# Loading the last pair's two wide tiles of x beside the next layer's first passes

## The chip, the cores and the metric

The kernel runs on one core of a Trainium2 chip. The metric is the device time of one execution in microseconds (us), lower is better. The engines have their own instruction queues and run them in order: TensorE (PE, matrix products into PSUM banks), VectorE (DVE), ScalarE (ACT), GpSimd (POOL, here mostly an issuer of DMAs) and SyncE (SP, an issuer of DMAs only).

## The reference

Two layers of a Fourier mixing and two of a gated feed-forward, in turn, on x of 2048 rows by 512 columns in float32:

```python
def mix(x):    # x: [S=2048, D=512]
    a = x @ dft_hid_re.T;  b = x @ dft_hid_im.T
    return dft_seq_re @ a - dft_seq_im @ b
def geglu(x):  # w_gate, w_up: [512, 1792], w_down: [1792, 512]
    return (gelu(x @ w_gate) * (x @ w_up)) @ w_down
for layer in range(4):
    n = (x - mean(x)) / sqrt(var(x) + 1e-5)      # per row
    x = x + (mix(n) if layer % 2 == 0 else geglu(n))
```

## The kernel before

**Products.** Each float32 operand is split into two halves, `hi` and `lo`: ACT copies `hi` (line 170), DVE subtracts to get `lo` (line 172). One product is then three matmuls of 128x128 by 128x512, `hi*hi`, `hi*lo` and `lo*hi` (lines 227, 228, 229). Large products are done by a seven-product scheme (names such as S1 to S4, T1 to T4, A11, A22, P1 to P7), so DVE also forms many sums and differences (lines 203, 207, 210, and 198 and 196 for negated splits).

**Stages.** A mixing layer takes the 2048 rows of the sequence transform in four blocks of 512 rows (`NB` is 4). For each block the stages A11, A12, S2 and S4 multiply the transform's tiles by the normalized rows; `s2` and `s4` run the last two. In the second mixing (layer 2) blocks are paired, (0, 1) and (2, 3), and the hidden transform is done once for a pair, as products P1 to P7 (`pair_product`). P1, P2, P4 and P7 run between the stages of the pair's blocks. The other three, P6, P5 and P3, four steps each, are the twelve entries of `PAIR_REST`. For the first pair they run beside stage S2 of block 2 (`s2` calls `pair_rest` at every second of its steps). For the last pair they are put on the list `spare`, and layer 3 takes them off one by one between its own first gate and up products (`up` calls `beside_mix` six times for each index n, so the twelve run beside the first two indices).

**The wide tiles.** The result of a pair product comes out transposed. DVE turns it back (`turned_into`, lines 865 and 210) and adds it to x, which lies in SBUF in a matching layout: one tile of 128x2048, 1 MB, for each block of a pair. The tile of the pair's first block is called `xwide` and that of the second `wide`. `pair_wide_load` fills one from DRAM with four DMAs of 256 KB on SP's queue (line 977), and `pair_out` writes it back with four on POOL's (line 980). Each name has one buffer. `xwide` is free long before the last pair. `wide` is also used for the normalized rows that the next layer turns: it is written by DVE (line 782), stored to a DRAM tile `t` by POOL (line 785), and `t` is fetched back in another layout by 16 small POOL DMAs for each half of the rows (line 796).

**What sets the order.** The code is written in the order of the work, and a scheduler places the instructions on each engine's queue with the help of its own timing model. All weights and transform tiles run through one stream (`items`, `load_next`, `take`): SP loads a tile into one of 98 slots `s` as soon as the slot's earlier tile has been read (line 350, or 1345 for prepared pieces of the gate and up weights, `wb`). A load on SP's queue that waits for its slot holds all loads behind it. Loads named `ws` are tiles of the sequence transform, `wq` pieces of the hidden transform for the pair products, `wb` and `wc` pieces of the feed-forward weights.

**The table that is changed.** `WIDE_AT = 14, 5` holds the step of `s2` and the step of `s4` of the last block at which `xwide` and `wide` are loaded. The other pair loads its two tiles in `pair_groups`, which the change leaves alone.

Of the kernel before, what the change touches and what calls it, by code (L numbers as in the profile page):

```python
# [20 lines left out]
NB = S // TB  # L21
# [5 lines left out]
MORE = 8  # L27
RAW = 4
FETCHING = 2
WIDE_AT = 14, 5  # L30
IN_ORDER = (3, 0),
HELD = {0: (1, 2, 3), 2: ()}
WARM = 12
# [33 lines left out]
def fnet_geglu(ctx: ExitStack, tc: tile.TileContext, x_in, ws, wh, wgu, wdn, wdc, whc, out):  # L67
# [53 lines left out]
    class Slots:  # L121
# [20 lines left out]
        def lend(self, tile, name):  # L142

            self.lent.add(name)
            self.free += [(tile[:, i * 512:(i + 1) * 512], name) for i in range(NT)]
# [17 lines left out]
    def behind(engine):  # L163
        return tc.issue_after(bank_read[engine].ins) if in_order[0] and engine in bank_read else ExitStack()
# [36 lines left out]
    def minus(out, a, b):  # L201
        with behind("DVE"):
            nc.vector.tensor_tensor(out, a, b, op=ALU.subtract)  # L203
# [652 lines left out]
    def moved(wide, outside, run):  # L856
        view = outside.rearrange("(j t) (p e) -> p t j e", t=32, e=P)
        for p in range(NT):
            v = wide[p * 32:(p + 1) * 32]
            run(v.rearrange("t (j e) -> t j e", e=P), view[p])  # L860
# [15 lines left out]
    def mix(layer):  # L876
# [58 lines left out]
        paired = {b for p in PAIRED.get(layer, ()) for b in p}  # L935
        by_pair = {b: p for p in PAIRED.get(layer, ()) for b in p}
        xu, xv, pair_banks, kept_p, pair_wide, late_v, sums_due, pair_now = {}, {}, {}, {}, {}, {}, [], [()]

        def arrived(b, m, c):
            if b not in paired:  # L940
                return
            t = cs.pop((m, c))
            if b == by_pair[b][0]:
                assert c not in (xv if m else xu)
                (xv if m else xu)[c] = t
                cs["P2" if m else "P1", c] = t
                return
            if m:
                cs["P4", c] = late_v[c] = t
            else:  # L950
                v = cs["P7", c] = sb.get(lasting=True)
                minus(v, xu[c], t)
                cs["u", c] = t
            if ("u", c) in cs and c in late_v:
                v = cs["P5", c] = cs.pop(("u", c))
                minus(v, v, late_v[c])
                read_once(c, late_v.pop(c))
                sums_due.append(c)

        def pair_sums():  # L960
            c = sums_due.pop(0)
            u, v = xu.pop(c), xv.pop(c)
            minus(u, cs["P5", c], u)
            with behind("DVE"):
                nc.vector.scalar_tensor_tensor(v, v, -1.0, u, op0=ALU.mult, op1=ALU.subtract)
            cs["P6", c], cs["P3", c] = u, v

        def pair_wide_load(b, n):
            pool = tpool if n else upool
            if b >= NB - 2:  # L970
                order = tc.issue_after(stream["last"].ins)
            else:
                order = ExitStack()
            assert not sb.out("z" if n else "x")
            pair_wide[n] = pool.tile([P, NT * D], F32, name="wide" if n else "xwide")
            with order:
                moved(pair_wide[n], xs[layer, b], lambda v, rows: nc.sync.dma_start(v, rows))
# [7 lines left out]
        def pair_product(name, k):  # L985
            bank = "P6" if name in ("P5", "P3") else name
            if bank not in pair_banks:
                pair_banks[bank] = [ps8.get() for _ in range(2)]
            ps = pair_banks[bank]
            (hi, lo), w = take()  # L990
            for c in range(2):
                cut = slice(c * P, (c + 1) * P)
                mm3(ps[c], (w[:, half[0]][:, cut], w[:, half[1]][:, cut]), (hi, lo), FIRST.get(name) == k, LAST[name] == k)
            sb.put(hi, lo, w)
            if LAST[name] == k:
                pair_ended(name, ps)
# [24 lines left out]
        def first_sum(c):  # L1021
            t, other = kept_p["P1"][c], kept_p["P2"][c]
            plus(t, t, other)
            turned_into(pair_wide[0], c, t)
            sb.put(t, other)

        def pair_rest(i):
            if sums_due:
                pair_sums()
            if i in FIRST_SUMS:  # L1030
                first_sum(FIRST_SUMS.index(i))
            pair_product(*PAIR_REST[i])
# [108 lines left out]
        def s2(b):  # L1141
            last = b == NB - 1
            if b == 0:
                lend("z")
                lend("x")
            cs.update(cs_next)
            cs_next.clear()
            for c in range(2):
                arrived(b, 0, c)
            chain = chain_banks.pop(b)  # L1150
            if b not in paired:
                x_banks(layer, b)
            one, three = [ps8.get() for _ in range(2)], [ps8.get() for _ in range(2)]
            sides[b] = one, three
            if last:
                late = later.pop("norms late", [])
                queue.extend(late + [None] * (FETCH_AT - len(late) if paired else 14) + [run for fetch in later.pop("fetches") for run in (None, fetch)])
            for j, (i, k) in enumerate(skewed(3)):
                if rest_beside(layer, b) and j % BESIDE == 0:
                    pair_rest(j // BESIDE)  # L1160
                    if j == len(skewed(3)) // 2:
                        stream["more"] = FURTHER
                if last and paired and j == WIDE_AT[0]:
                    pair_wide_load(NB - 2, 0)
                if i == 0:
                    six(chain, "T2", k, False, k == NK - 1)
                elif i == 1:
                    six(one, "T1", k, k == 0, k == NK - 1, "T12" if last else None)
                else:
                    six(three, "T3", k, k == 0, k == NK - 1)  # L1170
                if i == 0 and k == SEED_AT and b not in paired:
                    hid_banks[b] = x_seeded(b, range(2))
                if k < NK - 1:
                    continue
                if i == 0:
                    down_pieces(b, 1)
                    us[b] = [copied(p, b in paired) for p in chain]
                    ps8.put(*chain)
                    if b not in paired:
                        hid_banks[b] += x_seeded(b, range(2, NT))  # L1180
                for c in range(2):
                    if i == 1:
                        v = cs[1, 2 + c] = sb.get(lasting=b in paired)
                        plus(v, us[b][c], one[c])
                    elif i == 2:
                        plus(cs[1, 2 + c], cs[1, 2 + c], three[c])
                if i == 2:
                    for c in range(2):
                        arrived(b, 1, 2 + c)

        def s4(b):
            last = b == NB - 1
            if b == (1 if paired else NB - 4):
                sb.reclaim("z")
                if paired:
                    sb.reclaim("x")
            stream["more"] = 0
            one, three = sides.pop(b)
            u = us.pop(b)
            for j, (i, k) in enumerate(skewed(2)):  # L1200
                if last and paired and j == WIDE_AT[1]:
                    pair_wide_load(NB - 1, 1)
                if i == 0:
                    six(one, "B22", k, False, k == NK - 1, "22" if last else None)
                else:
                    six(three, "T4", k, False, k == NK - 1, "T34" if last else None)
                    if paired and b >= NB - 2:
                        for _ in range(-(-len(chores) // hid_left[0]) if chores else 0):
                            chores.pop(0)()
                        hid_left[0] -= 1  # L1210
                if k < NK - 1:
                    continue
                if i == 0:
                    down_pieces(b, 2)
                for c in range(2):
                    if i == 0:
                        v = cs[0, 2 + c] = sb.get(lasting=b in paired)
                        plus(v, u[c], one[c])
                    else:
                        plus(u[c], u[c], three[c])  # L1220
                        cs[1, c] = u[c]
                for c in range(2):
                    arrived(b, i, c if i else 2 + c)
            ps8.put(*one, *three)
# [653 lines left out]
```

## Time and profile before

| what | value |
|---|---|
| median of 3 runs | 1612.08 us (1611.62, 1612.08, 1616.12) |
| the profiled execution, own time | 1612.12 us |
| its span, first to last instruction | 1610.3 us |
| mean granted TensorE clock | 0.994 |
| PE busy | 1592.9 us, 99% of the span |
| DVE, ACT, POOL busy | 1189.7, 880.8, 315.6 us |
| DMA | 432.80 MB, mean 269 GB/s |
| the last pair's loads of x issued | `xwide` from 1112.8 us, `wide` from 1147.1 us |

The span is cut short by 1.8 us against the execution's own time, and that time equals the median within 0.1 us. A busy PE is not a PE at its peak: matmul records overlap, so stretches are compared below by how many matmuls were issued in them. Times in the profile are counted from the first instruction. "SPq" is SP issuing DMAs; a row's duration there is the time it spent issuing, not the time of the transfer.

### The profile page before, as it was taken

To read this page: it belongs to the slowest core of one execution; us is meant where nothing else is said; L and a number is where in the kernel's file an instruction comes from. 1 tells how busy PE (TensorE), PEld (TensorE's weight loads), DVE (VectorE), ACT (ScalarE), POOL (GpSimd) and SP (SyncE) were. 2 spreads that over 40 slices of the span, in tenths; PEclk is the share of its full clock that TensorE was granted. 3 is DMA by queue.
4 is the path that set the end of the run, shared out by engine and by line. 5 is a ranking of instruction groups with operands and counts; after the bars stand their busy time and mean duration, and the time that the engine had idled before them with its cause. 6 is when DMAs were issued, how large, how long until landed. Compare 5 with 4: busy or idle time off the path is not lost. (4 is left out here: it accounts for less than half of the span.)

```text
span 1610.3 us, 22765 instructions
## 1 busy us (share of the span) xinstructions
PE 1592.9 (99%) x6960; PEld 1311.8 (81%) x6960; DVE 1189.7 (74%) x2082; ACT 880.8 (55%) x1687; POOL 315.6 (20%) x533
## 2 busy tenths in 40 slices
PE   9999999999999999999999999999989999999999
PEld 7888888888888888888888888887768888888887
DVE  7997888878699784675878875998875556843574
ACT  8955565654767644656567543534542565433460
POOL 4122332341456102330040000022301000000000
PEclk9999999999999999999999999999889999999999
DMA  9888999976998899997786758789868958895445
GB/s 358 293 329 314 332 318 345 334 260 199 343 322 318 267 333 314 326 353 225 273 303 199 262 166 206 240 279 271 236 231 285 280 171 252 302 293 188 131 144 157
DMA packets 245019, 432.80 MB, mean 269 GB/s; under 512 B 29024, under 2 KB 72288, under 8 KB 243872
## 3 DMA queue, kind: packets, MB, share of 16 engines
q1 hardware_dynamic: 212208, 328.82, 63.6%
q0 software_dynamic: 30000, 100.43, 17.4%
q10 hardware_dynamic: 2688, 2.10, 0.5%
q8 instruction: 55, 0.90, 0.2%
q14 instruction: 68, 0.56, 0.1%
HBM read 333.97 MB, written 97.26 MB: 268 GB/s over the span
## 5 line engine op out<-in xcount | busy, mean ns | idle before, releaser
L228 PE MATMUL p<-s,s 128*128 128x512 f32 x2304 | 897.2, 390 | 0.6 <-DVE s L172 0.5
L229 PE MATMUL p<-s,s 128*128 128x512 f32 x2304 | 891.5, 390 | 3.5 <-DMA s<-wb 3.5
L227 PE MATMUL p<-s,s 128*128 128x512 f32 x2304 | 852.5, 391 | 8.3 <-ACT s L170 3.7
L170 ACT ACTIVATE s<-s 128x512 fp32r<-128x512 f32 (+1 forms) x852 | 480.4, 608 | 305.7 <-DVE s L203 69.7
L172 DVE TENSOR_TENSOR s<-s,s 128x512 fp32r<-128x512 f32 (+1 forms) x852 | 537.6, 663 | 119.5 <-ACT s L170 101.5
L227 PEld LDWEIGHTS p<-s,s 128*128 128x128 f32 x2304 | 434.2, 189 | 100.7 <-ACT s L170 4.7
L229 PEld LDWEIGHTS p<-s,s 128*128 128x128 f32 x2304 | 434.4, 189 | 94.1 <-DMA s<-wb 3.9
L228 PEld LDWEIGHTS p<-s,s 128*128 128x128 f32 x2304 | 434.1, 188 | 92.8 <-DVE s L172 2.2
L207 DVE TENSOR_TENSOR s<-s,p 128x512 f32<-128x512 f32 x211 | 142.3, 682 | 163.7 <-PE p L229 133.5
L203 DVE TENSOR_TENSOR s<-s,s 128x512 f32<-128x512 f32 (+1 forms) x399 | 234.6, 609 | 5.8 <-DMA s<-ws 3.2
L214 ACT ACTIVATE s<-p 128x512 f32<-128x512 f32 x234 | 135.6, 592 | 112.9 <-PE p L229 110.8
L1355 ACT ACTIVATE s<-s 128x512 f32<-128x512 f32 x84 | 52.8, 628 | 46.3 <-DVE s L207 45.9
L336 POOL DMA_DIRECT2D wb<-s x84 | 46.1, 550 | 86.2 <-ACT s L170 68.4
L1355 ACT ACTIVATE s<-p 128x512 f32<-128x512 f32 x28 | 16.7, 596 | 83.1 <-PE p L229 81.5
L689 ACT ACTIVATE s<-s,shift,rstd 128x512 f32<-128x512 f32 x61 | 48.8, 810 | 18.3 <-DVE shift L656 10.4
L1371 DVE TENSOR_TENSOR s<-s,p 128x512 f32<-128x512 f32 x56 | 38.3, 683 | 24.8 <-PE p L229 24.8
L980 POOL DMA_DIRECT2D x<-wide x8 | 5.2, 658 | 231.1 <-DVE wide L210 231.1
L221 ACT ACTIVATE p<-p 128x512 f32<-128x512 f32 x56 | 32.6, 584 | 31.6 <-PE p L229 31.4
L170 ACT ACTIVATE s<-xwide 128x512 fp32r<-128x512 f32 (+1 forms) x56 | 34.3, 618 | 27.9 <-DVE xwide L207 10.4
L210 DVE TENSOR_TENSOR s<-s,s 128x512 f32<-128x512 f32 (+1 forms) x61 | 36.4, 603 | 17.1 <-DMA s<-ws 12.4
L172 DVE TENSOR_TENSOR s<-xwide,s 128x512 fp32r<-128x512 f32 (+1 forms) x56 | 37.4, 676 | 15.3 <-ACT s L170 15.1
L666 POOL TENSOR_SCALAR rstd<-rstd 128x1 f32<-128x1 f32 x32 | 19.8, 619 | 108.1 <-ACT s L665 98.8
(96 smaller groups left out, 675.1 us busy)
## 6 DMA issues: line engine op xcount, KB each, us to landing
s<-ws SPq DMA_DIRECT2D x368, 256.0 KB, 5.0
s<-wb SPq DMA_DIRECT2D x294, 256.0 KB, 5.0
s<-wc SPq DMA_DIRECT2D x182, 256.0 KB, 4.4
wb<-s POOLq DMA_DIRECT2D x98, 256.0 KB, 4.6
s<-wq SPq DMA_DIRECT2D x56, 256.0 KB, 4.5
s<-x SPq DMA_DIRECT2D x52, 256.0 KB, 5.4
s<-wh SPq DMA_DIRECT2D x52, 256.0 KB, 5.6
wc<-s POOLq DMA_DIRECT2D x49, 256.0 KB, 5.4
```

The lines of the kernel that those rows point to most:

```text
L170: newest["ACT"] = nc.scalar.activation(hi, src, AF.Copy)
L172: newest["DVE"] = nc.vector.tensor_tensor(lo, src, f32(hi), op=ALU.subtract)
L203: nc.vector.tensor_tensor(out, a, b, op=ALU.subtract)
L207: bank_read["DVE"] = nc.vector.tensor_tensor(out, a, b, op=ALU.add)
L214: bank_read["ACT"] = nc.scalar.activation(v, src, AF.Copy)
L227: nc.tensor.matmul(ps, ah, bh, start=start, stop=False, skip_group_check=True)
L228: nc.tensor.matmul(ps, ah, bl, start=False, stop=False, skip_group_check=True)
L229: newest["PE"] = nc.tensor.matmul(ps, al, bh, start=False, stop=stop, skip_group_check=True)
L336: nc.gpsimd.dma_start(a, f32(t))
L689: nc.scalar.activation(z, x, AF.Identity, bias=shift, scale=rstd)
L1355: nc.scalar.activation(t, g, AF.Gelu_apprx_tanh)
L1371: nc.vector.tensor_tensor(t, t, v, op=ALU.mult)
```

## The change

The two loads leave `s2` and `s4` of the last block. `pair_rest` issues them instead, for the last pair alone: `WIDE_AT = 0, 2` now holds entries of `PAIR_REST`. At entry 0 the tile `wide` is loaded, at entry 2 the tile `xwide`. `wide` is first used when P6 ends (entry 3), `xwide` at entry 9.

```diff
-WIDE_AT = 14, 5
+WIDE_AT = 0, 2
...
         def pair_rest(i):
             if sums_due:
                 pair_sums()
+            if pair_now[0][1] == NB - 1 and i in WIDE_AT:
+                which = 1 - WIDE_AT.index(i)
+                pair_wide_load(pair_now[0][which], which)
             if i in FIRST_SUMS:
...
-                if last and paired and j == WIDE_AT[0]:
-                    pair_wide_load(NB - 2, 0)
...
-                if last and paired and j == WIDE_AT[1]:
-                    pair_wide_load(NB - 1, 1)
```

The number of instructions of each kind is the same before and after. In the rows below a name such as `s69_12677` is slot 69 and a running number, which differs between the two programs; `x2_2` and `x2_3` are the rows of x of the last pair's blocks in DRAM.

SP's queue in stage S2 of the last block, before:

```order
L350 DMA s94_12650<-wq0_181 128x512
L977 DMA xwide_12672<-x2_2_94 32x16x128 x4
L350 DMA s69_12677<-wq1_182 128x512
L350 DMA s86_12576<-ws 128x512
L350 DMA s18_12689<-ws3_0_3_176 128x512
```

and now:

```order
L350 DMA s94_12650<-wq0_181 128x512
L350 DMA s69_12672<-wq1_182 128x512
L350 DMA s18_12684<-ws3_0_3_176 128x512
L350 DMA s86_12576<-ws 128x512
L350 DMA s44_12819<-ws 128x512
```

The four loads of `xwide` no longer stand ahead of the transform tile in slot 86.

SP's queue in stage S4 of the last block, before:

```order
L350 DMA s76_12894<-ws 128x512
L977 DMA wide_12946<-x2_3_95 32x16x128
L350 DMA s34_12919<-ws 128x512
L977 DMA wide_12946<-x2_3_95 32x16x128 x3
L350 DMA s62_12966<-wq3_184 128x512
L350 DMA s83_12978<-wq2_183 128x512
```

and now:

```order
L350 DMA s76_12889<-ws 128x512
L350 DMA s34_12914<-ws 128x512
L350 DMA s62_12956<-wq3_184 128x512
L350 DMA s83_12968<-wq2_183 128x512
L350 DMA s66_12988<-wq3_184 128x512
```

The four loads of `wide` are gone from between the transform's last tiles and the weights of the pair products.

SP's queue where layer 3's weights are loaded, before:

```order
L1345 DMA s23_13111<-wb0_185 128x512
L350 DMA s2_13140<-wq0_181 128x512
L1345 DMA s96_13132<-wb1_186 128x512
L350 DMA s56_13146<-wq1_182 128x512
L350 DMA s27_13164<-wq2_183 128x512
L350 DMA s58_13182<-wq3_184 128x512
L350 DMA s85_13273<-wq0_181 128x512
L350 DMA s36_13296<-wc0_122 128x512
```

and now (one line less in the file from here on, so that line 1345 reads 1344):

```order
L1344 DMA s23_13101<-wb0_185 128x512
L1344 DMA s86_13123<-wb1_186 128x512
L350 DMA s2_13130<-wq0_181 128x512
L350 DMA s27_13154<-wq2_183 128x512
L350 DMA s56_13136<-wq1_182 128x512
L1344 DMA s96_13122<-wb1_186 128x512
L350 DMA s58_13172<-wq3_184 128x512
L977 DMA wide_13263<-x2_3_95 32x16x128 x4
L350 DMA s85_13268<-wq0_181 128x512
L350 DMA s36_13291<-wc0_122 128x512
```

The loads of `wide` now stand behind six other loads that follow the piece of `wb0` in slot 23, which layer 3's first product reads. The four of `xwide` follow eight loads later, behind the next `wq` pieces. The scheduler also moved some neighbours by a few places on PE, DVE and ACT between about 1117 and 1250 us; the largest such move on SP is a piece of `wb0` in slot 5, which now stands ahead of six loads that it stood behind.

## The prediction

> **What bounds the kernel now.** I read the page first, then PE's waits, then PE stretch by stretch, then the queues around each loss.
>
> ```profile
> span 1610.3 us, 22765 instructions
> ...
> PE 1592.9 (99%) x6960; PEld 1311.8 (81%) x6960; DVE 1189.7 (74%) x2082; ACT 880.8 (55%) x1687; POOL 315.6 (20%) x533
> ...
> PEclk9999999999999999999999999999889999999999
> ```
>
> PE is busy all along, so time can only be won where PE waits or its clock falls. The clock falls in two of the 40 slices, numbers 29 and 30 (1127 to 1208 us). PE's waits from 960 to 1300 us (total, times, longest):
>
> ```profile
> PE p L227 <- ACT s L170: 3.7, 2, 3.3
> PE p L229 <- DMA s<-wb: 3.5, 1, 3.5
> PE p L227 <- ACT s L214: 2.3, 1, 2.3
> PE p L227 <- DMA s<-wb: 1.6, 1, 1.6
> PE p L228 <- DVE s L172: 0.5, 1, 0.5
> ```
>
> These 11.6 us lie in three places, which I call A, B and C. The windows give PE's busy time with its matmul count, DVE's, the clock and the DMA share:
>
> ```profile
> 1124.24:1137.55 13.31, 9.50 (x23) 6.28 (x22) 9.50 (x21) 6.31 (x10) 7.34 (x12) 0.62 0.66 192
> 1137.55:1170.44 32.89, 32.89 (x147) 27.22 (x145) 31.05 (x52) 18.19 (x34) 9.30 (x17) 1.00 1.00 272
> 1170.44:1182.24 11.80, 6.67 (x19) 4.70 (x18) 10.28 (x18) 3.29 (x6) 0.00 (x0) 0.71 0.87 315
> 1191.78:1198.88 7.10, 4.84 (x15) 3.49 (x13) 5.90 (x10) 4.34 (x9) 0.00 (x0) 0.76 0.28 80
> ```
>
> A count includes one or two matmuls that straddle the edges. The undisturbed second window gives 32.89 / 145 = 0.227 us for a matmul. A holds 21 matmul starts, worth 4.76 us, so 8.55 of its 13.31 are lost; B holds 18 (4.08), so 7.72 are lost; C holds 13 (2.95), so 4.15 are lost. Together that is 20.4 us, more than the waits, because a slow clock follows them:
>
> ```profile
> 1124.01 0.61 PE L227 MATMUL p<-s,s 128*128 128x512 f32 x2
> 1127.88 1.22 PE L227 MATMUL p<-s,s 128*128 128x512 f32 x2 [3.25 <-ACT s L170]
> ...
> 1130.16 0.63 PE L228 MATMUL p<-s,s 128*128 128x512 f32 x1
> ...
> 1132.58 0.80 PE L228 MATMUL p<-s,s 128*128 128x512 f32 x1 [0.52 <-DVE s L172]
> ...
> 1172.47 0.47 PE L227 MATMUL p<-s,s 128*128 128x512 f32 x1 [1.65 <-DMA s<-wb]
> ```
>
> A record lasts 0.63 in the slow stretch behind A's wait, and 0.47 right behind the wait of 1.65, where the clock has not fallen yet.
>
> **The change, part by part.** SP issued the moved loads here:
>
> ```profile
> 1112.79 2.02 SPq L977 DMA_DIRECT2D xwide<-x  x4
> ...
> 1115.53 25.96 SPq L350 DMA_DIRECT2D s<-ws  x14
> ...
> 1148.03 1.49 SPq L977 DMA_DIRECT2D wide<-x  x3
> 1149.62 4.78 SPq L350 DMA_DIRECT2D s<-wq  x5
> ...
> 1160.88 3.27 SPq L1345 DMA_DIRECT2D s<-wb  x4
> ...
> 1166.99 5.06 SPq L1345 DMA_DIRECT2D s<-wb  x8
> ```
>
> The chain that ended last runs, in this part, through four transfers (start, duration):
>
> ```profile
> 1115.53 10.24 DMA s<-ws
> ...
> 1149.23 8.88 DMA s<-t
> ...
> 1158.40 6.38 DMA s<-t
> ...
> 1171.73 5.35 DMA s<-wb
> ```
>
> *A: xwide leaves S2.* The `ws` tile issued at 1115.53, right behind `xwide`, lands at 1125.77. DVE waits for it:
>
> ```profile
> 1120.59 0.14 DVE L651 TENSOR_SCALAR rstd<-mv 128x1 f32<-128x1 f32 x1
> 1125.86 0.69 DVE L210 TENSOR_TENSOR s<-s,s 128x512 f32<-128x512 f32 x1 [5.13 <-DMA s<-ws]
> ```
>
> The splits behind that sum are what PE waits for. The landings of `xwide` and of `wide` from their issues (shortest, median, longest):
>
> ```profile
> DMA to landing us min/median/max: 4.1/5.6/6.9
> ...
> DMA to landing us min/median/max: 4.7/6.9/11.8
> ```
>
> The first piece of `xwide` lands at 1112.8 + 4.1 = 1116.9, the last at 1114.3 + 6.9 = 1121.2: 1.45 us a piece, 5.8 for four. Without them the `ws` tile lands at about 1120.0; DVE is free for it at 1120.7. DVE's 5.13 goes, and with it PE's 3.25 and the slow stretch. What stays: the split that ended the 0.52 wait comes at 1132.5 - 5.1 = 1127.4, while PE, running on from 1124.24, is there 9 matmuls later, at 1126.3. So 1.1 of the 8.55 stays: A gives 7.4. Bounds: 0, if the small fetches of `t` hold the `ws` tile up as much, and 8.55. I take 7.4, since 5.8 is read from the pieces themselves.
>
> *B: wide leaves S4.* SP's queue was held by it:
>
> ```profile
> SPq L1345 <- DMA wide<-x: 4.0, 1, 4.0
> ```
>
> The last piece was issued at 1149.0 and landed 11.8 later, at 1160.8, just when SP issued the next `wb`. So the rush of `wb` loads from 1160.88 to 1172 starts late, and the one from which the chain goes over to PE lands at 1171.73 + 5.35 = 1177.08. That landing gains on three accounts. DVE and with it the slots, the stores and the fetches of `t` come 5.1 earlier, from A. The transfers lose 1 MB, at least 5.8 us by the price above (by the spread of the landings, 1151.8 to 1160.8 for the last three, up to 12). And four loads fewer stand ahead of it. Together 10.9 at least: it lands at 1166.2 or earlier. PE wants it at 1170.9 now, two matmuls behind the third window's start, and at 1163.5 with A's 7.4 gone. So 0 to 2.7 of B's 7.72 stay; I take 0.5, near the low end, because the price of 5.8 is the lower of the two: B gives 7.2. PE is then 14.6 early.
>
> *C follows.* PE waits for a copy that stands on ACT behind eight splits:
>
> ```profile
> 1179.23 0.58 ACT L221 ACTIVATE p<-p 128x512 f32<-128x512 f32 x1 [7.24 <-PE p L229]
> ...
> 1189.61 4.27 ACT L170 ACTIVATE s<-s 128x512 fp32r<-128x512 f32 x8
> ```
>
> They pile up because ACT sat for 7.24 us behind a copy that waited for PE in B. With B gone the pile goes, but DVE feeds the last of these splits, and DVE is the next bound. The feeding instruction, and DVE's waits just ahead of it:
>
> ```profile
> 1180.38 0.69 DVE L172 TENSOR_TENSOR s<-s,s 128x512 fp32r<-128x512 f32 x1 [0.99 <-ACT s L170]
> 1181.60 0.69 DVE L172 TENSOR_TENSOR s<-s,s 128x512 fp32r<-128x512 f32 x1 [0.53 <-ACT s L170]
> ...
> 1186.17 0.69 DVE L172 TENSOR_TENSOR s<-s,s 128x512 fp32r<-128x512 f32 x1 [1.47 <-ACT s L170]
> 1186.78 0.69 DVE L965 SCALAR_TENSOR_TENSOR s<-s,s 128x512 f32<-128x512 f32 x1
> ```
>
> It can come earlier by 5.13, these 3.0, and the 1.84 that DVE idles in the second window: 10.0, so it ends at 1177.5, and a split of 0.6 and the copy of 0.6 at 1178.7. PE, 14.6 early, wants the copy at 1192.0 - 14.6 = 1177.4, one matmul behind the fourth window's start. A wait of 1.3 stays; behind the 1.65 the clock had not fallen yet, so I charge no slow stretch. C gives 4.15 - 1.3 = 2.8 (bounds 0 and 4.15).
>
> *The new place.* Eight DMAs and some 4 us of issuing (2.02 for `xwide`, as much for `wide`) now stand on SP among loads for later products:
>
> ```profile
> 1188.00:1200.00 12.00, 9.74 (x36) 7.55 (x35) 10.60 (x19) 8.32 (x17) 0.00 (x0) 0.86 0.50 150
> 1209.16 1.25 DVE L210 TENSOR_TENSOR wide<-wide,s 128x512 f32<-128x512 f32 x2
> ```
>
> The DMA engines are half idle there, and the first sum into `wide` comes at 1209.16, near 1193 when PE and DVE run 16 early. `wide` is issued behind the `wb` rush, which ended at 1172 and ends near 1162 now (10.9 earlier); allowing a few more us for the `wq` loads between, and the longest landing, 11.8, it is there by about 1177. The cover is some 16 us. Cost 0; bounds 0 and 7.7, another B. On POOL nothing is moved past. I set 1.0 aside for waits as small as the 0.5 in the list.
>
> Sum: 7.4 + 7.2 + 2.8 - 1.0 = 16.4. Against the profiled execution's own 1612.1 (0.0 from the median), that is **1596 us**.
>
> [...]
>
> **The rivals.** *The chain holds B (1607 us).* PE gains A, arrives early and waits for `wb` all the more, since everything that the landing hangs on moves only with DVE: gain 5.1, 1607.0. For it: DVE is busy 31.05 of 32.89 in the second window and PE's operands come through it. Against it: SP's 4.0 wait on `wide`, which is no DVE time. Between this and the forecast lies a partial gain, 1600 to 1607.
>
> *The loads were not the cause (1612 us).* If the fetches of `t` and the other loads fill the same transfer time, the `ws` tile stays late and A whole; if the `wb` slots come free no sooner, so does B. For it: a margin of only 0.7 us (1120.0 against 1120.7) in A. Against it: a miss by 2 us would still give most of A, and in B SP waited for `wide` itself.
>
> *Slower (1618 us).* `wide` now loads behind the `wb` rush, and DVE stops at 1209.16 for it, with all later splits of layer 3 behind. Each us of lateness past the cover costs one. It decides when the landing takes 16 + 11.8 = 28 us or more, and it is slower than before past 44; 50 would give 1618. Nothing in the rows lands so late. The longest is 11.8.
>
> **How the numbers follow.** Forecast, 1592 to 1600: 0.62. Partial gain, 1600 to 1607: 0.19. All 20.4 gone, about 1591.7: 0.04. No change: 0.09. Slower: 0.06. A measurement of this kernel can tell about 0.3%, 4.8 us, from no change, so everything below 1607.2 counts as faster: 0.85. The range runs from 1591 (all lost time won) to 1606.
>
> **What would show it.** Right: the `ws` tile behind the `wq` lands in 3 to 6 us and DVE's 5.13 is gone; the clock row reads 9 in slice 29; SP no longer waits for `wide`; the `wb` waits of PE are under 1 us; ACT's copy holds PE for under 2. Wrong: a `wb` wait of 5 us or more again, a DVE wait on `ws` in the same place, or a wait of DVE for the load into `wide` or `xwide`. The forecast fails most easily at B, where two arrivals, each moved by several us, are subtracted.

## The result and the profile after

The changed kernel takes 1598.68 us (median of 1597.35, 1598.52, 1598.85 and 1601.68) against 1612.73 for the kernel before beside it: ratio 0.9912, 95% interval 0.9891 to 0.9933. That is 14.0 us less between the medians, where 16.1 were forecast. The page of the profiled execution (1597.35 us):

```profile
span 1595.5 us, 22757 instructions
...
PE 1584.5 (99%) x6960; PEld 1305.8 (82%) x6960; DVE 1188.8 (75%) x2082; ACT 881.3 (55%) x1687; POOL 314.3 (20%) x533
...
PEclk9999999999999999999999999999999999999999
```

The two slices with a lowered clock are gone, and PE is busy 8.4 us less with the same matmuls. The span is 14.8 us shorter. PE's waits in the profile after, from 1090 to 1230 us (total, times, longest):

```profile
PE p L227 <- ACT s L214: 2.2, 1, 2.2
PE p L229 <- DMA s<-wb: 1.1, 1, 1.1
PE p L228 <- DVE s L172: 1.0, 1, 1.0
PE p L227 <- ACT s L170: 0.4, 1, 0.4
PE p L227 <- ACT p L221: 0.2, 1, 0.2
```

The 11.6 us of before have become 4.9. In both, one wait of 0.4 for ACT (at 1108) lies outside the three places, so the prediction's sentence that all 11.6 lie in them is off by that much. The rows of PE's timeline behind these waits, in the profile after:

```profile
1127.30 0.50 PE L228 MATMUL p<-s,s 128*128 128x512 f32 x1 [0.95 <-DVE s L172]
...
1165.06 0.50 PE L229 MATMUL p<-s,s 128*128 128x512 f32 x1 [1.12 <-DMA s<-wb]
...
1166.93 0.50 PE L227 MATMUL p<-s,s 128*128 128x512 f32 x1 [0.21 <-ACT p L221]
...
1181.21 0.50 PE L227 MATMUL p<-s,s 128*128 128x512 f32 x1 [2.20 <-ACT s L214]
```

The first is what is left at A, the next two at B, the last at C. The chain that ended last (start, duration) shows two of the four transfers that the prediction listed, the `ws` tile and the last piece of `wb`, with another `wb` between them. Behind them stands the row of ACT's splits at C:

```profile
1114.32 5.51 DMA s<-ws
...
1151.27 8.32 DMA s<-wb
1159.67 5.35 DMA s<-wb
...
1173.29 1.67 ACT s L170 x3
...
1175.89 1.15 ACT s L170 x3
...
1177.46 1.62 ACT s L170 x3
```

The `ws` tile lands in 5.51 us instead of 10.24, at 1119.83. The piece of `wb` takes 5.35 as before, but lands at 1165.02 instead of 1177.08. The two fetches of `t` are gone from the chain. In their place stands an earlier piece of `wb`: SP issued the last piece at 1159.67, 0.08 us after that one had landed. What is left of B hangs on the row of `wb` loads itself.

For all profiles below, one measure is used: each step from the start of one matmul to the next, less the 0.227 us that a matmul takes undisturbed, summed over the place. By it the places lost, in us ("other" stands for all that was lost from 1195 to 1260):

| profile of | A | B | C | other, from 1195 to 1260 |
|---|---|---|---|---|
| before | 8.55 | 7.69 | 4.10 | |
| after | 1.23 | 1.89 | 2.47 | |
| e1, xwide moved alone | 1.69 | 10.11 | 4.13 | |
| e2, wide moved alone | 8.72 | 0.49 | 4.08 | 0.74 |
| e4, half of each moved | 4.10 | 8.73 | 1.12 | |
| e5, later splits | 1.79 | 4.94 | 0.96 | 2.11 |
| e6, later splits and swap | 1.54 | 1.63 | 1.71 | 2.32 |
| e7, both twice | 1.95 | 3.30 | 2.47 | 10.10 |
| e8, three entries later | 1.93 | 3.39 | 2.48 | |
| e9, after again | 0.64 | 2.16 | 4.08 | 0.49 |
| e10, swap | 1.29 | 1.11 | 2.56 | |
| e11, xwide twice | 0.62 | 2.31 | 2.47 | 2.56 |
| e12, wide twice | 1.23 | 3.39 | 3.93 | 5.42 |

In e3 the order of the matmuls differs too much for the three places to be matched. Of the 14.8 us, A gave 7.3, B 5.8, C 1.6. The profiles also differ ahead of 1090 us, by up to 2.6 us (e5), so a difference of spans is not the sum of a row.

### The profile page after: what moved, and what is told of

Read it like the earlier page. It is cut to its first block, busy times and chain, and to the rows that moved or that the text cites. A ratio compares the mean times of both kernels' runs of the same rounds, so it can differ in the third digit from the quotient of the medians.

```text
span 1595.5 us, 22757 instructions
## 1 busy us (share of the span) xinstructions
PE 1584.5 (99%) x6960; PEld 1305.8 (82%) x6960; DVE 1188.8 (75%) x2082; ACT 881.3 (55%) x1687; POOL 314.3 (20%) x533
## 5 line engine op out<-in xcount | busy, mean ns | idle before, releaser
L210 DVE TENSOR_TENSOR s<-s,s 128x512 f32<-128x512 f32 (+1 forms) x61 | 36.4, 602 | 19.5 <-DMA s<-ws 14.2
L782 DVE STREAM_TRANSPOSE wide<-s 128x512 f32<-128x512 f32 x30 | 21.3, 709 | 27.5 <-ACT s L689 22.1
```

## The experiments

My theory was that each load was paid where it stood: `xwide` at A, `wide` at B, and that the new place is free. The first four kernels move the loads in parts. Each ratio below is to the kernel before, run beside on the same chip.

**e1, only `xwide` moved**

```diff
-WIDE_AT = 0, 2
+WIDE_AT = None, 2
...
+                if last and paired and j == 5:     # in s4, as before
+                    pair_wide_load(NB - 1, 1)
```

> Only xwide goes to the new place; wide is loaded in the second mixing's last block as before. Theory (each load is paid where it stands): place A closes, ws lands in about 6 us, 7.4 us are gained there; B and C stay as before, so 1612.7 - 7.4 = about 1605. Rival 1 (B is the real limit and takes back what A gives, since its products of weights come from the same queue): SP's wait on wide grows by what A gave, 1610 to 1613. Rival 2 (the gain belongs to wide alone): 1612.

Measured: 1608.21 us, ratio 0.9976 (0.9966 to 0.9986), some 4 us gained, between the theory's 1605 and the first rival's 1610 to 1613. PE's waits in the profile of e1, same columns as above:

```profile
PE p L227 <- ACT s L170: 3.1, 2, 2.7
PE p L229 <- DMA s<-wb: 2.5, 1, 2.5
PE p L227 <- ACT s L214: 2.3, 1, 2.3
PE p L228 <- DVE s L172: 1.4, 1, 1.4
PE p L227 <- DMA s<-wb: 1.2, 1, 1.2
```

A closed as forecast (8.55 to 1.69), but B grew from 7.69 to 10.11. The chain of e1 says why:

```profile
1162.32 5.93 DMA s<-wq
1168.33 5.23 DMA s<-wb
```

The piece of `wb` lands at 1173.56, only 3.5 us earlier than the 1177.08 of before, while PE comes 6.9 earlier. B takes back part of what A gives as long as `wide` stands in front of it.

**e2, only `wide` moved**

```diff
-WIDE_AT = 0, 2
+WIDE_AT = 0, None
...
+                if last and paired and j == 14:    # in s2, as before
+                    pair_wide_load(NB - 2, 0)
```

> Only wide goes to the new place; xwide is loaded in the third step of the last block as before. Theory: A stays at 8.5 us lost (DVE waits 5 us for ws), SP's 4.0 us wait on wide is gone, B and C give the 5.8 + 1.6 that they gave in the changed kernel: about 1605. Rival 1 (B's lateness comes from A: the stores and fetches of t that A delays set when the slots of wb come free): B gives under 2 us, 1610 to 1612. Rival 2 (the gain is all wide's): 1599.

Measured: 1607.38 us, ratio 0.9965 (0.9952 to 0.9979), some 5.6 us gained, nearest to the theory. PE's waits in the profile of e2:

```profile
PE p L227 <- ACT s L170: 3.7, 2, 3.2
PE p L227 <- ACT s L214: 2.2, 1, 2.2
PE p L228 <- DVE s L172: 0.5, 1, 0.5
PE p L227 <- ACT p L221: 0.2, 1, 0.2
```

No wait on `wb` is left: moved alone, `wide` closes B (7.69 to 0.49), with A whole. So `wide` is what held B. C gave nothing here, where 1.6 had been expected. The two loads are not independent, as B's growth in e1 shows. Alone they give 3.9 and 5.6 us by their ratios, together 14.2 in the first measurement and 12.1 when the changed kernel was run again (e9). The 95% intervals of 12.1 and of the sum, 9.5, overlap, so these times do not show that both together give more than the sum.

**e3, the old places, on POOL's queue**

```diff
-lambda v, rows: nc.sync.dma_start(v, rows)
+lambda v, rows: (nc.gpsimd if b >= NB - 2 else nc.sync).dma_start(v, rows)
```

> The kernel before, both loads at their old places, but issued by POOL instead of SP: the same bytes at about the same time, not in SP's queue. If the transfers' share of the DMA engines is what costs: ws still lands some 10 us after its issue at A, 1609 to 1613. If standing in front of the others in SP's queue and its limit on loads under way is what costs: A and B shrink to 1 to 2 us each as in the changed kernel, 1599 to 1603. If POOL's own stores of t are held up behind them, the fetches of t come later and B stays: about 1605.

Measured: 1604.89 us, ratio 0.9955 (0.9942 to 0.9967). The number is the third one's, but this run doesn't tell the theories apart, since the loads did not stay where they were. The rows for the two tiles in the profile of e3 (shortest, median and longest issue in ns, first and last start):

```profile
L977 POOL DMA_DIRECT2D xwide<-x x4: 648/652/687, 1093.7 to 1095.9; - x4
L977 POOL DMA_DIRECT2D wide<-x x4: 648/650/660, 1158.5 to 1161.9; - x4
```

POOL was free and issued `xwide` 19 us earlier than SP had, and `wide` 11 us later, behind the fetches of `t`. Whether SP's order or the shared transfers cost more at A and B stays open.

**e4, half of each tile at each place**

```diff
+    pair_wide_load(NB - 2, 0, (0, 1))              # in s2
...
+    pair_wide_load(NB - 1, 1, (0, 1))              # in s4
...
-    pair_wide_load(pair_now[0][which], which)
+    pair_wide_load(pair_now[0][which], which, (2, 3))   # in pair_rest
```

> Two of the four transfers of each tile (half its bytes) at the old place, the other two at the new place. Theory (what is in front of ws and wb is paid byte for byte, nothing in reserve): half of the gain, about 1605 to 1606, DVE's wait on ws about 2.2 us. Rival 1 (some 3 us of reserve hide half a tile): 1599 to 1600. Rival 2 (what costs is the switch to the other kind of transfer, not its bytes): 1611.

Measured: 1605.91 us, ratio 0.9965 (0.9953 to 0.9978), as the theory said. DVE's wait on the `ws` tile is 2.4 against the 2.2 expected, and A loses 4.10, half of 8.55. The `ws` tile lands at 1122.21, between the 1119.83 of after and the 1125.77 of before: at this one point between all and nothing the price at A goes by the bytes. At B half of `wide` still costs 8.73, since PE comes there 5.0 us earlier than before; with all of it in front, e1 lost 10.11.

**e5 and e6, two attempts at what is left.** At C the copy stands on ACT behind a row of nine splits. Three of them are for P3, the last of the products, and e5's row has six. e5 makes the splits for P3 at most five products ahead; e6 also gives the slot that comes free last to another piece of `wb0`.

```diff
+            if at in close and at > n + CLOSE:     # close: the entries P3, CLOSE = 5
+                break
...
```

```diff
+            early.extend(sb.get(F32R) for _ in range(7))        # e6
+            early[1], early[2] = early[2], early[1]
```

> The changed kernel, with the splits for P3 made at most five products ahead, so that the three that stand last in front of the copy at C run behind it. Theory (C's wait is ACT's row of splits in front of the copy, 0.52 us each): the copy comes 1.6 us earlier, PE's 2.2 us wait falls to about 0.6, no fall of the clock: 1597 against 1598.7 of the changed kernel. Rival 1 (the copy waits for something else, or the next copy to a bank takes over the wait): 1598.7. Rival 2 (the three splits, made later, are late for their own products): 1600 or more.

> As e5, and the slot that comes free last among those of the first wb tiles is given to the second piece instead of the first. Theory (B's last 1.1 us is the second half of the first piece, whose slot comes free at 1155.9, 11 places behind the first half): B's waits fall under 0.5 us, together 1595.5 to 1596.5. Rival (the queue holds all wb tiles back by the same amount, and the next tile is as late): as e5, 1597.

Measured: e5 1601.74 us, ratio 0.9934 (0.9918 to 0.9950); e6 1599.59, ratio 0.9917 (0.9903 to 0.9930). Neither beats the changed kernel. PE's waits in the profile of e5 from 1090 to 1400 us (its lines from the split on are one higher, L1358 is the Gelu on ACT):

```profile
PE p L228 <- ACT s L171: 2.0, 3, 0.9
PE p L230 <- DMA s<-wb: 1.7, 1, 1.7
...
PE p L228 <- ACT s L215: 0.7, 1, 0.7
PE p L228 <- ACT s L1358: 0.7, 1, 0.7
```

C's wait fell from 2.2 to 0.7, as the theory said. But the loads stand in another order, ACT waits 8.3 us for a piece of x that layer 3 normalizes (3.0 in the changed kernel), and PE loses 2.1 us from 1241 to 1247. So the 1.5 us won at C were given back 60 us later. In this profile, one of e5's slower runs (1605.41), B lost 4.94 too, with a fall of the clock behind it (the run's mean granted clock is 0.999).

**e7, both tiles loaded twice at the new place**

```diff
                 pair_wide_load(pair_now[0][which], which)
+                moved(pair_wide[which], xs[layer, pair_now[0][which]], ...)   # the same load again
```

> The changed kernel, each tile loaded twice over at its new place: 16 transfers of 256 KB instead of 8. Theory (the new place has a reserve of 10 us and more, transfers there delay nothing that PE wants): 1598.5 to 1600. Rival (the queue there is as full as at the old places, and 5 to 6 us more in front of the products' weights reach PE, once or twice): 1604 to 1610.

Measured: 1611.04 us, ratio 0.9991 (0.9980 to 1.0002): my theory was wrong and the rival right, by more than it said. The chain of e7, and below it ACT's wait and PE's:

```profile
1228.95 7.06 DMA s<-wb
1240.72 1.90 DMA s<-x
...
1246.75 0.49 ACT s L1355
```

```profile
ACT s L663 <- DMA s<-x: 10.9, 1, 10.9
```

```profile
PE p L227 <- ACT s L1355: 6.5, 1, 6.5
...
PE p L227 <- DMA s<-wq: 1.7, 1, 1.7
```

SP's later loads come some 11 to 13 us later, the piece of x (`s<-x`) among them. It lands at 1242.6 instead of 1230.75. ACT, in order, waits for it, the Gelu behind it is late, and PE stops 6.5 us. With the slow clock behind it (the run's mean granted clock is 0.998) that is 8.2 of the 10.1 us in the table; the other 1.9, at 1203, goes to a late `wq` load. DVE waited 3.1 us for the second load of `xwide` as well, but the chain does not pass through that wait. The same row of the changed kernel shows that there was no spare time at all in that piece:

```profile
ACT s L663 <- DMA s<-x: 3.0, 1, 3.0
```

ACT waits for it there too, and waited 1.9 us even in the kernel before. Only the time between ACT's work on that piece and the moment PE wants the Gelu behind it keeps PE running.

**e8, three entries later**

```diff
-WIDE_AT = 0, 2
+WIDE_AT = 3, 5
```

> The changed kernel with both loads three entries later in the row of products (entries 3 and 5 instead of 0 and 2): wide is issued at about 1182 and lands by 1192, before its first use at 1195.7; xwide is issued at about 1194 and lands at about 1204, 5 us behind its first use at 1198.6. Theory (DVE has 8 us and more of reserve there): DVE waits about 5 us, PE 0 to 2, 1599 to 1601. Rival (DVE's wait goes on to PE in full): 1604.

Measured: 1600.54 us, ratio 0.9925 (0.9912 to 0.9938). The time is the theory's, the premise isn't: `xwide` was issued at 1180.9, not 1194, and landed at 1194.4, ahead of its first use at 1201.1. No load was late, so what lateness costs wasn't tried. Three entries more or less make no difference that these runs can tell.

**e9 to e12, on one chip.** e9 is the changed kernel again, e10 has the swap of e6 alone, e11 and e12 load `xwide` or `wide` alone twice.

> The changed kernel once more, unaltered, beside the next three on one chip. B lost 1.9 us in its first profile and 3.3 to 3.4 in two kernels that are the same up to there: theory (B's remaining loss varies from run to run with the landings of wb): 1597.5 to 1600, B between 1.9 and 3.5 us, A about 1.2 to 1.9, C's gap 2.59. If B's 1.9 is fixed, A, B and C come out at 1.2, 1.9 and 2.5 again.

> The changed kernel, with the slot that comes free last among those of the first wb tiles given to the second piece instead of the first (the part of e6 without the later splits). Theory (the last half of the first piece is all that keeps PE at B, and what e6 lost at 1237 to 1243 came from the later splits): B's wait on wb goes, B loses about 0.5 to 1, nothing is lost at 1237 to 1243: 1 to 2 us under e9, about 1597. Rival (the next tile in the queue is as late): as e9.

> The changed kernel, xwide alone loaded twice over at its new place (4 more transfers, half of what e7 added). e7 lost 12 us: every later load of SP's queue came 11 us later, the piece of x that ACT wants at about 1231 too, ACT waited 10.9 us for it and PE 6.5 behind ACT. Theory (the price is bytes in the queue beyond a reserve of some 3 to 5 us): the piece of x lands 5 to 6 us later, ACT waits 7 to 9 us, PE loses 2 to 4: 1601 to 1603. Rival (DVE's wait on xwide itself is what costs): as e7, 1606 to 1611.

> As e11 with wide instead of xwide, 20 us ahead of its use: the same bytes in the same queue, but xwide lands once. Theory (bytes in the queue): the same as e11, 1601 to 1603. Rival (only xwide's own landing counts, wide has 20 us of reserve): as e9, 1598 to 1600.

Measured: e9 1600.13 us, ratio 0.9925 (0.9913 to 0.9937); e10 1600.82, ratio 0.9929 (0.9914 to 0.9944); e11 1602.82, ratio 0.9944 (0.9931 to 0.9957); e12 1602.27, ratio 0.9941 (0.9926 to 0.9957).

e9 lands 1.4 us over the first measurement, inside both intervals. Its waits are nearly those of the first profile (A lost 0.64, less than the 1.2 to 1.9 expected), but C lost 4.08 and not 2.47. PE's timeline in the profile of e9:

```profile
1181.55 0.50 PE L227 MATMUL p<-s,s 128*128 128x512 f32 x1 [2.20 <-ACT s L214]
...
1182.34 0.54 PE L227 MATMUL p<-s,s 128*128 128x512 f32 x1
1182.68 0.63 PE L228 MATMUL p<-s,s 128*128 128x512 f32 x1
1183.11 0.63 PE L229 MATMUL p<-s,s 128*128 128x512 f32 x1
```

The same wait of 2.20 in the same program was followed by half a clock here (records of 0.63 us; mean granted clock 0.76 from 1178.95 to 1185.99) and by none in the first profile (1.00 from 1178.62 to 1184.06).

e10 did what was meant at B. PE's waits in its profile have no `wb`, and B lost 1.11 where e9 lost 2.16:

```profile
PE p L227 <- ACT s L214: 1.6, 1, 1.6
PE p L228 <- DVE s L172: 1.5, 2, 1.0
PE p L227 <- ACT s L170: 0.7, 2, 0.4
PE p L227 <- ACT p L221: 0.2, 1, 0.2
```

Its median is no lower than e9's. Its runs reach from 1596.98 to 1604.93, so a gain of 1 us can't be told.

e11 and e12 came out within the theory's range, 2.7 and 2.1 us over e9 by the medians. Both intervals overlap that of e9 at the edge, so it is the profiles that carry the reading. ACT's wait for the piece of x in the profile of e12, and what it does to PE:

```profile
ACT s L663 <- DMA s<-x: 8.0, 1, 8.0
```

```profile
PE p L227 <- ACT s L1356: 3.6, 1, 3.6
```

In e11 the same two are 5.7 and 1.4, below the 7 to 9 and 2 to 4 expected, and DVE waits for `xwide` in neither. Which of the tiles is doubled doesn't decide; what is added in front of the piece of x does. (The profile of e12 is its slowest run, 1607.8.) So 2 MB at the new place cost PE next to nothing there (nothing in the first profile, 0.5 us at 1241 in e9), one more costs 2 to 3 us, two more 11 (1611.04 against 1600.13).

## Why the prediction was right, and where not

- *A, forecast 7.4.* Right: 7.3 in the first profile, 7.9 in e9. The `ws` tile was to land at 1120.0 and landed at 1119.83; DVE's 5.13 became 0.5. Of A 1.1 was to stay, and 1.23 did in the first profile. e1 shows it with `xwide` alone and e4 with half the price for half the bytes.
- *B, forecast 7.2.* The mechanism was right and the size was off: 5.8 in the first profile, 5.5 in e9, 4.3 in e8. Both arrivals were placed well (PE wanting `wb` at 1163.5, the landing by 1166.2 against a measured 1165.02; in e8 it was 1167.4). The step that failed is "I take 0.5, near the low end" of the 0 to 2.7 that could stay: the landing left a wait of 1.12, one of 0.21 followed, and 1.9 to 3.4 stayed in the six profiles (after, e7, e8, e9, e11, e12) that share this part of the program row by row. In three of them (e7, e8, e12) that is over the 2.7 as well. The 7.2 holds only with A open (e2).
- *C, forecast 2.8.* Mis-sized, and for the wrong reason. The step of 2.64 us at C (before) is 2.59 in the changed kernel, with or without either load (2.65 in e1, 2.59 in e2). Neither load set it. In e4 the step is 1.24, and why stays open. I took DVE as the next bound, feeding the splits by 1177.5; DVE was done at 1177.0, and ACT's own row of splits, 0.52 us each, held the copy until 1180.58. The 1.6 that C gave is the slow clock that followed in the profile of before and not in that of after. In e9 it followed again, and C gave nothing. So C's share of the total was luck.
- *The new place, forecast 0 with 1.0 set aside.* Nothing was lost there in the first profile and 0.49 in e9, and `wide` was there at 1175.8 (forecast 1177), 20 us ahead of its use. But the reserve wasn't the cover of 16 us in front of that use, as I put it. It was what stood behind in SP's queue, the piece of x, and e11 shows it spent after one more MB. I looked at who waits for the moved loads, not at who waits for the loads behind them.
- *The sum.* 7.3 + 5.8 + 1.6 = 14.7, the 14.8 of the span, against 16.4. Where the clock falls at C, as in e9, it is 7.9 + 5.5 + 0 - 0.5 = 12.9, and the run came out at 1599.83.
- *The rivals.* "The chain holds B" is what e1 does: `wb` follows DVE and the transfers, and PE's early arrival turns into a wait. With `wide` gone too it held only 1.9 to 3.4 us of it. "The loads were not the cause" fell with e1 and e2. "Slower" didn't come by DVE's wait on a late `wide`; e7 shows the way it would have come, through the piece of x.
- *DVE's idle time.* The forecast let the 1.84 us that DVE idled go with C. That holds for 1.57 of them: it was a wait for ACT at 1165.46, not for a fetch, and the profile after has no such wait. Whether the fetches on POOL's queue and SP's loads hold each other up isn't shown: e3, meant for the two queues, left it open.
- *What was to show it.* Seen: `ws` in 3 to 6 us, no 5.13, nines in the clock row, no long wait of SP for `wide` (1.2 at most). Just missed: PE's `wb` wait under 1 (1.1) and ACT's copy under 2 (2.2).

## What to carry to other kernels

A load that is moved to where nobody needs it soon is paid by whoever waits for the loads behind it in the same queue (in e7 ACT waited 10.9 us for the piece of x, and PE stopped 6.5): look for the tightest of those before calling the new place free. Two stalls in a row don't add up when the second one's supply doesn't move with the first. Closing the first alone can feed the second, as B's growth from 7.69 to 10.11 in e1 shows. A gain that is read from one profile may be a clock that happened not to fall (after the same wait of 2.20 us, C lost 2.47 in the first profile of the changed kernel and 4.08 in e9): split a loss into waiting and slow matmuls, and believe the waiting.

## What the runs showed of the hardware

A PE gap of the same length did or didn't lower the clock. At C, PE waited 2.2 us in seven profiles, and a matmul started 2.59 us after the one ahead of it (2.60 in e9). The clock fell behind it in e2, e9 and e12, where C lost 4.08, 4.08 and 3.93, and not in the first profile of the changed kernel, e7, e8 and e11, where C lost 2.47 or 2.48.

Each fall at C slowed seven or eight matmuls to 0.43 us instead of 0.227 and cost 1.4 to 1.6. In the profile of before the granted clock was 0.50 from 1126.92 to 1137.16, from 1174.70 to 1181.53 and from 1195.18 to 1198.59, and 1.00 between these stretches; the last of them stands behind the step of 2.64 at C.

So 2.59 was enough three times in seven. What decides it is not shown.
